# Loading the upper heads of each batch from a second DMA queue, in linear attention followed by a multiplicative FFN

## Chip, cores and metric

The kernel runs on one core of a Trainium2 chip. The metric is the time of one execution on the device, in microseconds (us); several runs give a median. One execution is also taken with the hardware profiler, and its trace is what the views below are read from.

## What is computed

The reference is linear attention with the feature map elu(x) + 1, followed by a feed-forward block in which two projections are multiplied. There are 8 batches, 8 heads, 576 positions and a head size of 64, so 4608 tokens of width 512; the hidden width is 1024. All inputs and the output are float32.

```python
def phi(x):
    return np.where(x > 0, x, np.exp(x) - 1.0) + 1.0
q_p, k_p = (phi(q), phi(k))
kv = np.einsum('bhsd,bhse->bhde', k_p, v)
z = np.sum(k_p, axis=2)
num = np.einsum('bhsd,bhde->bhse', q_p, kv)
den = np.einsum('bhsd,bhd->bhs', q_p, z)[..., None] + 1e-06
# heads are put side by side: x is 4608 x 512
a = x @ w1
b = x @ w2
h = a * b @ w3
return (h @ w_out).astype(np.float32)
```

## The kernel before, in words

Each of q, k and v of one batch is loaded into one tile of 128 partitions: heads 0 to 3 lie in partitions 0 to 63 and heads 4 to 7 in partitions 64 to 127, with nine positions of each of four heads on a partition (2304 contiguous bytes per head). `load_qkv` writes such a tile with two DMAs, one for each half of the partitions (`hh` is 0 or 1), 576 KB each. For batch 0 alone the work is cut finer: `part` 0 and 1 take two heads of each half, 288 KB per DMA. All these loads are issued from SP. Their tiles come from a pool of five (`ld`), which also holds two tiles of w3; a load waits until the tile that lay in its buffer has been read.

From a batch's tiles, ScalarE (ACT) takes the exponential, VectorE (DVE) makes phi (tiles `kphi`, `qphi`), and ACT casts v into `vt`. TensorE (PE) then forms k'v and its sums (`kv_unit`, tile `kvp`). qphi is transposed by DMA (`qt_load`, tile `qt`, two DMA transposes per batch, issued from SP), PE multiplies it with kv (`nat_unit`, tile `nd`), DVE divides (`xn`, and `xnr` for the 64 positions left over), and `xt_load` transposes the result by DMA, again from SP, into `xt`, the tokens' transposed layout that the FFN reads. Batch 0 is transposed on PE instead.

w3 and w_out are multiplied into one matrix on the chip at the start (`w3_tr`, `wf_mm`). The FFN runs over nine chunks of 512 tokens: eight `f_unit`s each (a and b, multiplied into `ab`) and four `o_unit`s, whose results (`o_sb`, four buffers) GpSimd (POOL) stores with two DMAs of 128 KB each. The weights w1, w2, w_out and w3 are loaded from POOL's queue as well, with a cast to bfloat16; the first of these DMAs is made to wait for the second part of k of batch 0 (`after(wl[0], first_loads[3])`), and the load of q of batch 1 for the second DMA of w3.

The order of all this is written out by hand: strings such as `NEXT` name the units in program order. F and O are the FFN's units, K and Q the steps of phi, V the cast of v, T `qt_load`, KV and N the attention's matrix products, X `xt_load`, and Lk, Lq and Lv the loads for the batch after next. Each engine runs its own instructions in this order.

```python
NEXT = """KV F0 Lk Ke0 F1 Ks0 Ks1 O0 N0 Ke1 Ks2 Ks3 F2 N1 O1 Lq N2 F3 N3 X0 Qe0 Qs0 Qs1
          O2 N4 X1 F4 Qe1 Qs2 O3 Lv F5 Qs3 V T F6 F7"""
```

Each DMA takes one of eight semaphores of its kind in turn (eight for the DMAs that SP and ACT issue together, eight for POOL's), so a DMA also waits until the eighth DMA before it has landed.

Of the kernel before, what the change touches and what calls it, by code (L numbers as in the profile page):

```python
# [18 lines left out]
def kernel(  # L19
# [11 lines left out]
    nc = tc.nc  # L31
# [34 lines left out]
    mm_ps = ctx.enter_context(tc.tile_pool(name="mm_ps", bufs=4, space=bass.MemoryType.PSUM))  # L66
    at_ps = ctx.enter_context(tc.tile_pool(name="at_ps", bufs=2, space=bass.MemoryType.PSUM))

    nc.scalar.preload_act_table_set("natural_log_exp_and_others")

    ident = consts.tile([P, P], BF16)
    make_identity(nc, ident)
# [19 lines left out]
    def load_qkv(name, src, b, part=None):  # L92

        if part is None or part == 0:
            raw[name, b] = ld.tile([P, 4, X], F32, tag="ld", name=f"{name}32")
        n, h0 = (4, 0) if part is None else (2, 2 * part)
        for hh in range(2):
            ins = nc.sync.dma_start(  # L98
                out=raw[name, b][hh * TP:(hh + 1) * TP, h0:h0 + n, :],
                in_=src[b, hh * 4 + h0:hh * 4 + h0 + n].rearrange("h (p j) d -> p h (j d)", j=NJ))  # L100
        return ins
# [196 lines left out]
    def after(ins, first):  # L298
        tc.add_manual_dep(ins.ins, first.ins.name, mybir.DependencyInfo(
            mybir.DependencyClass.Sync, mybir.DependencyReason.SCHED_ONLY), reason="load order")  # L300

    def load_w12(x):
        cols = slice(x * WQ, (x + 1) * WQ)
        return [nc.gpsimd.dma_start(  # L304
            out=d[:, :, cols], in_=w.rearrange("(c p) n -> p c n", p=P)[:, :, cols])
            for d, w in ((w1_sb, moe_w1), (w2_sb, moe_w2))]
# [39 lines left out]
    def load(name, b, part=None):  # L346
        return load_qkv(name, src[name], b, part)

    first_loads = [load(n, 0, i) for i in range(NI) for n in "kqv"]
    wl = [i for x in range(4) for i in load_w12(x)]  # L350
    after(wl[0], first_loads[3])
    wl += [load_wo(0), load_wo(1)]
# [131 lines left out]
```

## Time and profile before

| | |
|---|---|
| median of 3 runs | 312.65 us (312.0 to 315.04) |
| the profiled execution's own time | 312.29 us |
| its span, first to last instruction | 310.5 us |
| PE busy | 242.8 us (78%) |
| DVE busy, ACT busy | 151.6 us, 134.6 us |
| mean granted TensorE clock | 0.932 |
| moved by DMA | 51.57 MB; q1 (SP) 36.64 MB, q0 (POOL) 14.69 MB |

Times in the views are us from the start of the span unless marked ns. A row of a timeline gives start, duration, engine, line, what is written from what, and in brackets the idle time before it and what ended it. In the DMA view, q1 is the queue of SP's DMAs and q0 that of POOL's; a row has packets, MB and the time that the packets took as a share of 16 DMA engines over the stretch. Packets of one engine can overlap, so the shares may add up to over 100%. Bytes are counted as written: a cast to bfloat16 counts half of what it reads. The page's row of DMA bytes shows 173 to 261 GB/s in each of the first 27 slices of 7.76 us.

### The profile page before, as it was taken

Reading aid. Unit: us, or ns where it says so; the run is one execution under the profiler, and the core shown is the slowest. Engines: PE = TensorE matmul, PEld = TensorE weight load, DVE = VectorE, ACT = ScalarE, POOL = GpSimd, SP = SyncE. Lnnn points to the kernel's source line nnn. Section 1 sums busy time; section 2 is a strip of 40 time slices with the busy share of each in tenths; the row PEclk is TensorE's granted clock in tenths of the full one; section 3 lists DMA queues with packets and bytes.
Section 4 is the critical chain, followed back from the end, with each engine's and each line's share of the span. In section 5 each row is a group of like instructions: output and inputs, shape, how many; then the busy total and the mean of one; then the engine's idle time right before and its main releaser. Section 6 shows DMA issues by size and latency. Waiting matters only on the chain.

```text
span 310.5 us, 3924 instructions
## 1 busy us (share of the span) xinstructions
PE 242.8 (78%) x1430; PEld 116.0 (37%) x1450; DVE 151.6 (49%) x291; ACT 134.6 (43%) x187; POOL 52.4 (17%) x103
## 2 busy tenths in 40 slices
PE   0248999595197439399789999959999999999960
PEld 0223455242044114144334544524455444444420
DVE  0555404638347903379557579647755441222200
ACT  3477377725425405237505555542553333333330
POOL 2273300013000002011102112111202202203150
PEclk9999999979689958979959999997999999999995
DMA  7999999999989999999999999990781713303250
GB/s 173 229 225 198 209 237 223 214 193 261 216 170 215 211 218 187 216 204 209 204 238 213 212 221 245 218 198 9 145 108 38 144 36 68 68 2 83 52 117 20
DMA packets 56499, 51.57 MB, mean 166 GB/s; under 512 B 35744, under 2 KB 40864, under 8 KB 56480
## 3 DMA queue, kind: packets, MB, share of 16 engines
q1 hardware_dynamic: 46592, 36.64, 60.5%
q0 software_dynamic: 9888, 14.69, 22.9%
q8 instruction: 11, 0.18, 0.3%
q14 instruction: 8, 0.07, 0.1%
HBM read 38.80 MB, written 9.44 MB: 155 GB/s over the span
## 4 chain that ended last, share of the span: by engine, by line
PE 57%; DMA 31%; DVE 3%; SPq 2%; ACT 2%; issue 2%; POOL 1%; POOLq 0%; ACTq 0%; DVEq 0%
PE o_ps L286 18%; PE a_ps L267 18%; PE b_ps L267 17%; DMA qt<-qphi 9%; DMA xt<-xn 7%; DMA v<-in_v_dram 6%; DMA w3b<-in_moe_w_dram 4%; DMA w_sb<-in_moe_w_dram 3%; DMA k<-in_k_dram 3%; PE nd L179 3%; PE kvp L141 2%; SPq L98 1%; ACT vt L127 1%; DVE xn L186 1%; POOL w_sb L304 1%
## 5 line engine op out<-in xcount | busy, mean ns | idle before, releaser
L267 PE MATMUL a_ps<-xt,w_sb 128*128 128x512 bf16 x280 | 76.1, 397 | 18.3 <-DMA xt<-xn 18.2
L273 DVE TENSOR_TENSOR ab<-a_sb,b_ps 128x512 bf16<-128x512 f32 x72 | 49.3, 686 | 79.3 <-PE b_ps L267 74.8
L267 PEld LDWEIGHTS <-w_sb 128*128 128x128 bf16 x560 | 54.9, 101 | 85.0 <-issue 18.6
L267 PE MATMUL b_ps<-xt,w_sb 128*128 128x512 bf16 x280 | 75.9, 396 | 0.0
L291 POOL DMA_DIRECT2D out_dram<-o_sb x72 | 37.7, 528 | 225.8 <-ACT o_sb L289 225.8
L272 ACT COPY a_sb<-a_ps 128x512 f32<-128x512 f32 x72 | 42.0, 585 | 76.5 <-PE a_ps L267 73.5
L286 PE MATMUL o_ps<-wf_sb,ab 128*128 128x512 bf16 x272 | 69.0, 391 | 1.0 <-issue 0.2
L289 ACT COPY o_sb<-o_ps 128x512 f32<-128x512 f32 x36 | 21.0, 585 | 65.4 <-PE o_ps L286 63.4
L286 PEld LDWEIGHTS <-ab 128*128 128x128 bf16 x288 | 28.4, 101 | 33.2 <-issue 4.0
L114 DVE TENSOR_SCALAR e<-e 128x1152 bf16<-128x1152 bf16 x32 | 14.9, 467 | 29.7 <-ACT e L113 29.4
L179 PE MATMUL nd<-kv,qt 128*128 128x130 bf16 (+1 forms) x144 | 15.5, 230 | 14.6 <-DMA qt<-qphi 11.1
L117 DVE SCALAR_TENSOR_TENSOR qphi<-q,e 128x576 bf16<-128x576 f32 x32 | 23.2, 754 | 0.5
L117 DVE SCALAR_TENSOR_TENSOR kphi<-k,e 128x576 bf16<-128x576 f32 x32 | 23.0, 754 | 0.4
L113 ACT ACTIVATE e<-k 128x1152 bf16<-128x1152 f32 x16 | 18.6, 1166 | 8.1 <-DMA k<-in_k_dram 8.1
L127 ACT CAST vt<-v 128x1152 bf16<-128x1152 f32 x16 | 18.0, 1168 | 8.1 <-DMA v<-in_v_dram 8.1
L179 PEld LDWEIGHTS <-qt 128*128 128x128 bf16 (+1 forms) x144 | 10.9, 105 | 26.4 <-DMA qt<-qphi 13.1
L186 DVE TENSOR_TENSOR xn<-nd,r 128x512 bf16<-128x512 f32 x28 | 19.4, 692 | 1.0
L113 ACT ACTIVATE e<-q 128x1152 bf16<-128x1152 f32 x16 | 18.5, 1165 | 2.7 <-DMA q<-in_q_dram 2.7
L209 PE MATMUL tp<-ident,qphi 128*128 128x128 bf16 x18 | 2.3, 310 | 17.4 <-DVE qphi L117 17.4
L334 PE MATMUL wf_ps<-wo_sb,w3t 128*128 128x512 bf16 x61 | 14.8, 379 | 1.2 <-ACT w3t L329 1.0
L184 DVE TENSOR_SCALAR r<-nd 128x8 f32<-128x8 f32 (+1 forms) x36 | 5.7, 159 | 18.6 <-PE nd L179 18.6
L141 PE MATMUL kvp<-vt,kphi 64*128 64x130 bf16 x288 | 10.9, 224 | 3.3 <-ACT vt L127 3.3
(45 smaller groups left out, 96.9 us busy)
## 6 DMA issues: line engine op xcount, KB each, us to landing
out_dram<-o_sb POOLq DMA_DIRECT2D x72, 128.0 KB, 3.0
q<-in_q_dram SPq DMA_DIRECT2D x14, 576.0 KB, 11.8
k<-in_k_dram SPq DMA_DIRECT2D x14, 576.0 KB, 8.0
v<-in_v_dram SPq DMA_DIRECT2D x14, 576.0 KB, 9.8
w_sb<-in_moe_w_dram POOLq DMA_DIRECT2D x8, 256.0 KB, 9.6
w3b<-in_moe_w_dram POOLq DMA_DIRECT2D x8, 256.0 KB, 13.7
k<-in_k_dram SPq DMA_DIRECT2D x4, 288.0 KB, 6.0
q<-in_q_dram SPq DMA_DIRECT2D x4, 288.0 KB, 7.2
```

What stands on the lines that cost most here:

```text
L113: nc.scalar.activation(out=e[:, hs], in_=x[:, hs], func=AF.Exp)
L117: nc.vector.scalar_tensor_tensor(out=dst[:, h // 2, :, h % 2, :], in0=x[:, h].rearrange("p (j d) -> p j d", d=D), scalar=1.0, in1=e[:, h]. ...
L127: (copy or nc.scalar.copy)(out=vt[:, i, :, :, 0:D].rearrange("p j u d -> p u j d"), in_=raw["v", b][:, 2 * i:2 * i + 2].rearrange("p u (j ...
L141: nc.tensor.matmul(kvp[:, hh, i * KVW:(i + 1) * KVW], ph["k", b][rows, i, j].rearrange("p u d -> p (u d)"), vt[rows, i, j].rearrange("p u ...
L179: nc.tensor.matmul(nd[0:n, hp // 2, (hp % 2) * KVW:(hp % 2 + 1) * KVW], qts[b][:, hp, m * P:m * P + n], t[:, hp].rearrange("p h e -> p (h ...
L186: nc.vector.tensor_tensor(out=dst.rearrange("p (a x) e -> p a x e", a=2), in0=v4[:, :, :, 0:D], in1=r[0:n].unsqueeze(3).to_broadcast([n, 2 ...
L267: nc.tensor.matmul(ps, w[:, kc, f * P:(f + 1) * P], xt[:, 4 * c:4 * c + 4, kc, :], start=(kc == 0), stop=(kc == KC - 1))
L272: nc.scalar.copy(out=a_sb, in_=a_ps)
L273: nc.vector.tensor_mul(out=abs_[c][:, f, :], in0=a_sb, in1=b_ps)
L286: nc.tensor.matmul(o_ps, ab[:, f, m * P:(m + 1) * P], wf_sb[:, f, :], start=(f == 0), stop=(f == FC - 1))
L289: nc.scalar.copy(out=o_sb, in_=o_ps)
L291: nc.gpsimd.dma_start(out=out[b * S:(b + 1) * S, :].rearrange("(p j) n -> p j n", j=NJ)[:, j, :], in_=o_sb[i * TP:(i + 1) * TP, :])
```

## The change

The first DMA of each pair (heads 0 to 3) stays on SP. The second (heads 4 to 7, partitions 64 to 127) is issued from POOL's queue, except for part 0 of batch 0, where ACT issues it. The load of ACT's table is moved behind ACT's three DMAs.

```diff
-    nc.scalar.preload_act_table_set("natural_log_exp_and_others")
...
         for hh in range(2):
-            ins = nc.sync.dma_start(
+            ins = (nc.sync if hh == 0 else nc.scalar if (b, part) == (0, 0) else nc.gpsimd).dma_start(
                 out=raw[name, b][hh * TP:(hh + 1) * TP, h0:h0 + n, :],
                 in_=src[b, hh * 4 + h0:hh * 4 + h0 + n].rearrange("h (p j) d -> p h (j d)", j=NJ))
         return ins
...
     first_loads = [load(n, 0, i) for i in range(NI) for n in "kqv"]
+    nc.scalar.preload_act_table_set("natural_log_exp_and_others")
     wl = [i for x in range(4) for i in load_w12(x)]
     after(wl[0], first_loads[3])
```

`load_qkv` returns the second DMA of its pair, so both manual dependencies (of the first weight on k, and of q of batch 1 on w3) now hang on a DMA of POOL's own queue.

The first place is the start of the program on POOL, from the last memset to the first stores. Before (`w_sb`, `wo_sb` and `w3b` are the weights):

```order
L87 MEMSET vt 128x36
L304 DMA w_sb<-in_moe_w_dram 128x4x256 x8
L310 DMA wo_sb<-in_moe_w_out_dram 128x4x512 x2
L319 DMA w3b<-in_moe_w_dram 128x1024 x8
L236 COPY kv<-kvn 128x8x64
L237 COPY kv<-kvz 128x8
L291 DMA out_dram<-o_sb 64x512 x72
```

The same place of the changed kernel, whose lines from `load_qkv` on count one less:

```order
L86 MEMSET vt 128x36
L97 DMA k_111<-in_k_dram 64x2x576
L97 DMA q_114<-in_q_dram 64x2x576
L97 DMA v_117<-in_v_dram 64x2x576
L303 DMA w_sb<-in_moe_w_dram 128x4x256 x8
L309 DMA wo_sb<-in_moe_w_out_dram 128x4x512 x2
L318 DMA w3b<-in_moe_w_dram 128x1024 x8
L235 COPY kv<-kvn 128x8x64
L236 COPY kv<-kvz 128x8
L97 DMA q_299<-in_q_dram 64x4x576
L97 DMA k_302<-in_k_dram 64x4x576
L97 DMA v_305<-in_v_dram 64x4x576
```

Three loads of batch 0 come ahead of the weights, and the upper halves of batch 1 (`q_299`, `k_302`, `v_305`) behind all of them.

The second place is one later chunk (a pass over `NEXT`) on SP, before:

```order
L98 DMA k_1336<-in_k_dram 64x4x576 x2
L98 DMA q_1418<-in_q_dram 64x4x576 x2
L198 DMA_TRANSPOSE xt<-xn 128x16x128
L198 DMA_TRANSPOSE xt<-xnr 128x4x64
L98 DMA v_1510<-in_v_dram 64x4x576 x2
L161 DMA_TRANSPOSE qt<-qphi 128x18x64 x2
```

The same chunk on SP with the change:

```order
L97 DMA k_1336<-in_k_dram 64x4x576
L97 DMA q_1418<-in_q_dram 64x4x576
L197 DMA_TRANSPOSE xt<-xn 128x16x128
L197 DMA_TRANSPOSE xt<-xnr 128x4x64
L97 DMA v_1510<-in_v_dram 64x4x576
L160 DMA_TRANSPOSE qt<-qphi 128x18x64 x2
```

And on POOL with the change, where there were stores alone before:

```order
L97 DMA k_1336<-in_k_dram 64x4x576
L290 DMA out_dram<-o_sb 64x512 x4
L97 DMA q_1418<-in_q_dram 64x4x576
L290 DMA out_dram<-o_sb 64x512 x4
L97 DMA v_1510<-in_v_dram 64x4x576
L97 DMA k_1615<-in_k_dram 64x4x576
```

On SP one DMA of each pair is gone, and the transposes stand behind half as many loads. On POOL the other halves stand between the stores of the output, in program order.

## The prediction

> **What bounds the kernel now.** I read the page first, for its busy rows, its DMA row and its queues.
>
> ```profile
> span 310.5 us, 3924 instructions
> ...
> PE 242.8 (78%) x1430; PEld 116.0 (37%) x1450; DVE 151.6 (49%) x291; ACT 134.6 (43%) x187; POOL 52.4 (17%) x103
> ...
> DMA  7999999999989999999999999990781713303250
> ...
> q1 hardware_dynamic: 46592, 36.64, 60.5%
> q0 software_dynamic: 9888, 14.69, 22.9%
> ```
>
> The DMA row stands at 9 tenths or more from the second slice to the 27th, that is up to 210 us. The two queues' packets take 60.5% + 22.9% of 16 engines' span, against PE's 78% busy. Next I cut the span at the places where PE starts a new stage, and asked for the busy time of each.
>
> ```profile
> 24.70:63.00 38.30, 33.11 (x214) 16.67 (x217) 15.90 (x26) 24.91 (x34) 5.02 (x10) 1.00 1.15 216
> 63.00:84.50 21.50, 11.03 (x70) 5.04 (x71) 11.06 (x25) 9.19 (x11) 4.25 (x8) 0.83 1.10 228
> 84.50:113.80 29.30, 18.10 (x120) 8.66 (x121) 18.40 (x37) 8.94 (x13) 0.00 (x0) 0.85 1.01 198
> 113.80:146.90 33.10, 27.60 (x152) 12.47 (x156) 18.60 (x37) 14.64 (x19) 4.18 (x8) 0.88 1.09 208
> 146.90:176.40 29.50, 26.50 (x153) 12.34 (x156) 18.35 (x37) 13.96 (x20) 4.18 (x8) 0.88 1.02 212
> 176.40:199.70 23.30, 23.20 (x151) 11.42 (x152) 18.09 (x36) 13.19 (x18) 4.18 (x8) 1.00 1.09 231
> 199.70:228.60 28.90, 25.39 (x155) 11.99 (x158) 18.30 (x36) 13.29 (x18) 4.18 (x8) 0.94 0.66 124
> 228.60:300.40 71.80, 71.35 (x369) 33.31 (x376) 23.00 (x41) 22.84 (x40) 15.53 (x30) 1.00 0.34 67
> ```
>
> The columns are the stretch, its length, busy time and instructions of PE, PEld, DVE, ACT and POOL, the granted clock, the DMA share and GB/s. The row 176.40 to 199.70 is one whole chunk that nothing held up: 23.2 us busy of 23.3, clock 1.00. The chunks at 113.8, 146.9 and 199.7 do the same work (151 to 155 PE instructions) in 33.1, 29.5 and 28.9 us; they lose both idle time and clock. Behind 228.6 PE is busy for 71.35 of 71.8 us, and nothing there can be gained from DMA; ahead of it, DMA limits. What PE waited for is in the view of waits (total us, times, longest).
>
> ```profile
> PE a_ps L267 <- DMA xt<-xn: 18.2, 2, 9.5
> ...
> PE nd L179 <- DMA qt<-qphi: 11.1, 6, 3.5
> ...
> PE kvp L141 <- ACT vt L127: 3.3, 3, 2.6
> ```
>
> The chain of waits shows how long each such transfer was under way.
>
> ```profile
> 42.44 18.18 DMA v<-in_v_dram
> ...
> 74.57 9.86 DMA xt<-xn
> ...
> 102.56 11.12 DMA xt<-xn
> ```
>
> The 18.18 us are those of v of batch 1, most of it queue: its 1.18 MB alone are 5.4 us at the rate found below. A stall costs a second time, since PE comes out of it slow. In the timeline, four matmuls of 512 columns just before the qt stall at 127 us, and just behind it:
>
> ```profile
> 122.96 1.04 PE L267 MATMUL a_ps<-xt,w_sb 128*128 128x512 bf16 x4
> ...
> 131.91 1.91 PE L267 MATMUL a_ps<-xt,w_sb 128*128 128x512 bf16 x4
> ```
>
> 1.91 us instead of 1.04 for the same work.
>
> Why are the transfers late? In a stretch in which q1 alone worked, with loads that fill one half of the partitions at a time (50 to 53 us):
>
> ```profile
> q1 hardware_dynamic: 300, 0.65, 104.7%
> ```
>
> 300 packets, 0.65 MB in 3 us, 217 GB/s; q1's packets follow one another without a gap (104.7%). That looks like a full machine, but it isn't one. From 44 to 47 us POOL's queue still worked on w3:
>
> ```profile
> q1 hardware_dynamic: 251, 0.55, 56.2%
> q0 software_dynamic: 174, 0.30, 52.8%
> ```
>
> q1 kept 251 of its 300 packets, and 0.30 MB of q0 came on top: 0.85 MB in 3 us, 284 GB/s. Between 77 and 78 us loads on q1 met stores of the output on q0:
>
> ```profile
> DMA packets 157, 0.38 MB, mean 377 GB/s; under 512 B 22, under 2 KB 22, under 8 KB 157
> ...
> q1 hardware_dynamic: 98, 0.23, 63.6%
> q0 software_dynamic: 59, 0.15, 47.5%
> ```
>
> 377 GB/s, of which q1 has 0.23 MB, no less than alone (0.65 / 3 = 0.22). So **217 GB/s is what one queue gets with loads into one half, not what the 16 engines can move.**
>
> **The change, part by part.** Loads are 42 DMAs of 576 KB and 12 of 288 KB, 28.3 MB. At 217 GB/s they take 130 us in one queue. With the halves in two queues I expect between 217 GB/s (nothing gained) and 377 (the best stretch above); I take 340, between the 284 and the 377 and nearer to the latter, because in the 377 row q1 lost nothing, while the other has a q0 that reads twice what it writes. That makes 83 us. Transposes are the other load on q1. With almost nothing beside them (83 to 86 us):
>
> ```profile
> q1 hardware_dynamic: 1995, 0.49, 94.9%
> ```
>
> 0.49 MB in 3 us, 165 GB/s. The transposes of a batch, 590 KB of qt and 590 KB of xt, take 1.18 / 0.165 = 7.2 us. A chunk loads three tiles of 1.18 MB: before, 3.54 / 0.217 = 16.3 us, with the transposes 23.5, and with 1.05 MB of stores partly beside them more than the 23.3 us that PE needs. After: 3.54 / 0.34 + 7.2 = 17.6 us, and some 21 with stores at 0.34. **DMA then needs less than PE, and the queue empties within each chunk.** At 284 it is 12.5 + 7.2 + 3.7 = 23.4, just even.
>
> What a transpose takes with an empty queue stands in the DMA view of 215 to 235 us (issues, median us to landing):
>
> ```profile
> qt<-qphi SPq DMA_TRANSPOSE x2, 5.7
> xt<-xn SPq DMA_TRANSPOSE x1, 5.5
> ```
>
> So the sum, by stages:
> - *Start, to 24.7 us.* The loads of batch 0 moved at 238 GB/s, a little above the 217 because the short halves overlap at their borders:
>
> ```profile
> DMA packets 1161, 2.38 MB, mean 238 GB/s; under 512 B 128, under 2 KB 128, under 8 KB 1161
> ```
>
> 3.54 MB take 14.9 us at this rate, 10.4 at 340; the end comes 4.5 us earlier. The weights wait for k on POOL for 11.2 us, and ACT takes the last v at 18.83:
>
> ```profile
> POOL w_sb L304 <- DMA k<-in_k_dram: 11.2, 1, 11.2
> ...
> 18.83 1.17 ACT L127 CAST vt<-v 128x1152 bf16<-128x1152 f32 x1 [0.27 <-DMA v<-in_v_dram]
> ```
>
> On POOL k now stands first, and the weights follow when it has landed, some 4 us sooner. But three queues share the first loads, so that the first q may land no earlier. Bounds 0 and 5 us; I take 3, nearer to the 4.5.
> - *24.7 to 63.* The halves of batch 1 on SP no longer wait for w3; those on POOL stand behind the last weight, as q's second half did before. v lands well before PE asks: the 3.3 us of `kvp` go. Bounds 0 and 4; 3.
> - *63 to 84.5.* Without the v stall the first `o_unit` runs at full clock:
>
> ```profile
> 63.68 3.47 PE L286 MATMUL o_ps<-wf_sb,ab 128*128 128x512 bf16 x8
> ```
>
> Its eight matmuls take 3.47 us; at the full clock, by the pair above, about half, so 1.7 us are saved. The xt transpose takes 5.5 us instead of 9.86, so 4.4 are saved. Together 6.
> - *84.5 to 113.8.* xt 11.12 to 5.5 us: 5.6. The rest of that stall stays, since PE has work for only 11.12 - 9.5 = 1.6 us from the issue on.
> - *113.8 to 146.9, 146.9 to 176.4, 199.7 to 228.6.* The last two fall to the 23.3 us of the clean chunk: 6.2 + 5.6. Of the 9.8 us of the first I leave out two slow starts of 1.7 us: one behind the xt stall that stays, one in case the first qt still comes late. 6.4, together 18.2.
>
> 3 + 3 + 6 + 5.6 + 18.2 = 35.8. Against it I set 3 us for transposes that meet q0's loads on the engines, which the trace of before shows only with stores: at 82 to 83 us the transposes got 0.07 MB, against 0.49 / 3 = 0.16 alone.
>
> ```profile
> q1 hardware_dynamic: 260, 0.07, 35.3%
> q0 software_dynamic: 73, 0.19, 57.3%
> ```
>
> A delay of half a 576 KB load (2.7 us at 217) at each of the two xt stalls would be 3 us in all; bounds 0 and 10 (2.7 us at the two xt stalls and half of that in the three chunks that wait for qt). So 32.8 us are gained: 310.5 - 32.8 = 277.7 us of span, and with the 1.8 us that lie outside it (the execution's 312.29 - 310.5) **279.5 us**. The profiled execution is 0.4 us below the median of 312.65; that changes nothing.
>
> Costed at nothing: POOL's issues, 24 more of them. The nearest row is that of the weights (mean 798 ns for 512 rows of the tile; a load has 256):
>
> ```profile
> L304 POOL DMA_DIRECT2D w_sb<-in_moe_w_dram x8 | 6.2, 798 | 11.2 <-DMA k<-in_k_dram 11.2
> ```
>
> 24 x 0.8 = 19 us, hidden by POOL's idle time (52.4 us busy of 310.5). If that cover went, stores would be late first, and `o_sb` has four buffers. Behind an upper half that waits for its buffer on POOL stand the stores of the next `o_unit`; the buffer is freed by DVE or ACT steps that come ahead of that unit in program order, so PE doesn't wait for them. q's upper half now follows O1's stores, a third of a chunk later than the lower half, but is used a chunk later. ACT's new issues and its table load lie ahead of its first exponential:
>
> ```profile
> 0.74 1.40 SPq L98 DMA_DIRECT2D k<-in_k_dram  x2
> ...
> 0.74 1.28 ACT L69 ACT_TABLE_LOAD   x1 [0.74 <-PEq L468]
> ...
> 6.10 1.16 ACT L113 ACTIVATE e<-k 128x1152 bf16<-128x1152 f32 x1 [4.07 <-DMA k<-in_k_dram]
> ```
>
> 0.74 + 3 x 0.7 + 1.28 = 4.1 us, against 6.10; two us of cover are left, of which a k landing 1 us sooner takes one.
>
> **A rule against it.** The Trainium skill, "SBUF — State Buffer", section "Can I just issue two DMAs to hit both halves?", says no: two DMAs into the two halves at once were measured only 6% above one. Its section on the port swizzle in the same page puts 64 partitions at about 218 GB/s, and the trace agrees (217 in one queue). The 284 and 377 GB/s above speak against the first rule where the second DMA is in another queue, though no row of before has two loads of opposite halves in two queues. By the 6%, the time would be that of the first rival.
>
> **The rivals.**
> - *Nothing gained in the rate* (a queue more, the same engines). For it: q1's packets already fill the engines' time, 104.7%. Against it: the 377 GB/s. Then the rate stays between 217 and the 238 of the start, the waits above (18.2 + 11.1 + 3.3 us) shrink by a tenth at most, some 3 us, and the start gains an issue or two of 0.7: 307 to 312 us. Chance 0.09. The Trainium skill's rule above is this case.
> - *Half the gain*, a rate like the 284: queues empty only at the end of a chunk. The v wait goes, xt and qt land 2 to 3 us sooner in place of 4 to 5, and half of the clock loss stays: some 20 us, 287 to 296. Chance 0.22.
> - *Slower:* transposes starve. On SP a transpose had to wait only for loads issued ahead of it; now q0 can hold an upper v and the next k, issued later, which the engines serve in turn with it. If the engines' rate stays at 217 and the turn is by packets (256 bytes against 2304), a transpose ends only with q0's 1.18 MB, 5.4 us later. It decides as soon as such a delay is longer than what the halved loads ahead of it save (2.7 us); over the two xt and four qt, the clean chunk's among them, that is 6 x 2.7 = 16 us, and 328 us. The row at 82 us speaks for the turn, the 377 against the fixed rate. Chance 0.06.
>
> **Chances and range.** Forecast (266 to 287) 0.63, half 0.22, nothing 0.09, slower 0.06. The upper end reaches through the second rival to 300. The lower takes the start at 5, no loss to q0, the first of the three chunks clean, all the idle time of the second stage (38.3 - 33.1 = 5.2 in place of 3), and xt stalls too short for the clock to fall: 279.5 - 2 - 3 - 3.4 - 2.2 - 3.4 = 265.5, rounded to 266. A run of this kernel tells 1% (3 us) from nothing. Faster by over that 0.87, within it 0.07, slower 0.06.
>
> **What would show it.** Right: in the row of stretches, over 300 GB/s wherever loads run; 23.3 us for the chunk in which N0 waited; xt in 5.5 to 7 us; v no longer in the chain; a DMA row with gaps ahead of 200 us. Wrong: 217 GB/s with both queues busy; q1 transposes whose landing grows; PE idle behind `o_ps` because POOL sits on a load.

## Result and the profile after

The change made the kernel slower: 324.46 us (322.23 to 328.27, four runs) against 313.16 us of the kernel before in the same runs (312.0 to 315.04), a ratio of 1.033 with a 95% interval of 1.025 to 1.042. Times here and below are medians of all runs, while ratios compare the means of those runs that lie within 1.5% of the fastest of their kernel (one run of `first_only`, at 433.95 us, lies far outside). The forecast was 279.5 us, with a range of 266 to 300; it was wrong, and in the sign too. The profiled execution took 324.24 us. From the page of the changed kernel, the rows that answer to those shown of before:

```profile
span 322.5 us, 3954 instructions
...
DMA  7999999999899999996999999699177260321324
...
q0 software_dynamic: 13152, 27.96, 42.7%
q1 hardware_dynamic: 40016, 22.48, 39.8%
```

The bytes were moved as intended: q0 now carries 27.96 MB in place of 14.69, q1 22.48 in place of 36.64. The DMA row stands at 9 tenths in 24 of its first 28 slices, now of 8.06 us each: up to 226 us in place of 210. The limit that was to go away lasts longer than before. The view of waits shows where PE pays:

```profile
PE nd L178 <- DMA qt<-qphi: 29.6, 10, 8.2
...
PE a_ps L266 <- DMA xt<-xn: 8.7, 2, 4.4
...
PE w3p L327 <- DMA w3b<-in_moe_w_dram: 3.3, 1, 3.3
```

The wait for xt fell from 18.2 to 8.7 us, as forecast. The wait for qt rose from 11.1 to 29.6 us and ate twice that, and a wait for w3 (before its transposition on PE, `w3p`) rose from 0.6 to 3.3 us. In the DMA view of the whole span, the median time from issue to landing of the 14 transposes into qt says the same thing in one row. First before, then after:

```profile
qt<-qphi SPq DMA_TRANSPOSE x14, 7.1
```

```profile
qt<-qphi SPq DMA_TRANSPOSE x14, 11.1
```

The chain of waits names the worst of them. In the kernel before it has three over 5 us:

```profile
121.62 10.05 DMA qt<-qphi
...
149.90 6.62 DMA qt<-qphi
...
199.94 9.95 DMA qt<-qphi
```

In the changed kernel it has six, of 8.29 to 18.97 us; the three longest:

```profile
61.48 12.51 DMA qt<-qphi
...
89.64 18.97 DMA qt<-qphi
...
186.21 14.04 DMA qt<-qphi
```

The following table puts the first `kvp` matmul of batches 1 to 7 side by side, from the timelines (us from the span's start). The last column is an experiment from below, `two_dma`, for comparison.

| mark | before | after | `two_dma` |
|---|---|---|---|
| batch 1 | 61.9 | 64.4 | 58.0 |
| batch 2 | 91.2 | 96.4 | 81.4 |
| batch 3 | 121.3 | 128.6 | 102.6 |
| batch 4 | 146.9 | 155.5 | 124.4 |
| batch 5 | 176.4 | 186.1 | 149.1 |
| batch 6 | 199.7 | 218.6 | 172.5 |
| batch 7 | 228.5 | 244.5 | 195.9 |
| last copy into `o_sb` | 300.4 | 316.4 | 267.7 |
| end of span | 310.5 | 322.5 | 277.9 |

The change loses 1 to 3 us in each stage up to batch 5, and 9.2 us from batch 5 to 6: the chunk that nothing held up before (23.3 us) now takes 32.5. These are two rows of the stretches of the changed kernel (columns as in the prediction):

```profile
186.10:218.60 32.50, 25.07 (x153) 11.81 (x156) 18.30 (x36) 13.31 (x18) 5.51 (x10) 0.89 0.99 174
218.60:244.50 25.90, 23.52 (x151) 11.32 (x152) 18.11 (x36) 13.30 (x18) 4.20 (x8) 1.00 0.62 127
```

In the first, the DMA share is 0.99 and yet only 174 GB/s are moved, less than the 217 of one queue. The engines are full, of something slow. The second is shorter than before (25.9 against 28.8 us). 4 us come back behind the last store (4.2 us from the end of its issue to the end of the span, against 8.2), for which I have no cause.

**What the engines do then.** I cut the transposes at 89.64, the 18.97 us of the chain, into pieces of 3 us. One from the middle, 96 to 99 us, and one from behind the loads, 105 to 108 us (packets, MB, share of 16 engines):

```profile
q0 software_dynamic: 135, 0.55, 95.3%
q1 hardware_dynamic: 137, 0.04, 10.2%
```

```profile
q1 hardware_dynamic: 1804, 0.51, 122.1%
q0 software_dynamic: 19, 0.05, 6.4%
```

The two queues get the same number of packets, 135 and 137 (112 and 116 in the piece before, 144 and 141 in the next; from 90 to 93 us it was even 143 to 35). But a packet of q0 carries 0.55 MB / 135 = 4.1 KB on average (in the trace 4608 bytes, two rows, with some packets of 4 bytes between them), and one of the transposes 256 bytes. So q1 moves 0.04 MB in 3 us; as soon as q0 is empty it makes 1804 packets and 0.51 MB in the same time. The Trainium skill, "DMA: Bandwidth & Descriptors", section "Queues, rings and completion order", says that each DMA engine serves the queues that have work in turn and changes at packet borders; the equal counts here agree. Whether the packets that the profile counts are those of that page isn't shown.

The stall at 186.21 us looks different. From 189 to 192 us:

```profile
q0 software_dynamic: 78, 0.29, 103.4%
q1 hardware_dynamic: 434, 0.11, 34.4%
```

Here the transposes get more than five packets for one of q0, and still only 0.11 MB in 3 us (0.10 in the next 3 us). That transposes are slow while q0's loads are under way holds for both stalls; turns one for one are shown for the longest alone.

What q0 has to do at that moment stands in the timeline of POOL and of SP:

```profile
88.16 0.62 POOL L97 DMA_DIRECT2D k<-in_k_dram  x1
90.47 0.62 POOL L97 DMA_DIRECT2D q<-in_q_dram  x1 [1.69 <-issue]
```

```profile
87.18 12.94 SPq L160 DMA_TRANSPOSE qt<-qphi  x2
100.22 3.32 SPq L97 DMA_DIRECT2D k<-in_k_dram  x1
```

From 86.29 to 91.1 us POOL issues five upper halves, 2.95 MB, of batches 3 and 4; the first step that reads any of them, the exponential of k of batch 3, starts at 111.69 us. They stand beside the transposes of batch 2, issued at 87.18, for which PE waits. In SP's single queue they would have come behind. SP itself sits in the two transposes for 12.94 us (3.82 before) and issues its next loads so much later, so that here the opposite halves do not run together. SP's issuing alone doesn't explain the slow transposes: it ends at 100.12 us, and from 100.1 to 102 us the counts are still 91 and 91.

At the start the same turn meets the weights. Between 24 and 27 us:

```profile
q1 hardware_dynamic: 255, 0.55, 85.8%
q0 software_dynamic: 255, 0.12, 30.8%
```

Batch 1's lower halves no longer wait behind w3 on their own queue, and take 255 of 510 packets beside the weights, whose packets are the small ones here (0.12 MB / 255 = 0.5 KB). PE's first matmul on w3 waits 3.3 us for it.

### The profile page after: what moved, and what is told of

It reads as the page before. It is cut to its first block, busy times and chain, and to the rows that moved or that the text cites. A ratio compares the mean times of both kernels' runs of the same rounds, so it can differ in the third digit from the quotient of the medians.

```text
span 322.5 us, 3954 instructions
## 1 busy us (share of the span) xinstructions
PE 247.6 (77%) x1430; PEld 117.9 (37%) x1450; DVE 151.2 (47%) x291; ACT 134.6 (42%) x187; POOL 67.6 (21%) x127
## 3 DMA queue, kind: packets, MB, share of 16 engines
q0 software_dynamic: 13152, 27.96, 42.7%
q1 hardware_dynamic: 40016, 22.48, 39.8%
## 4 chain that ended last, share of the span: by engine, by line
PE 48%; DMA 37%; issue 4%; DVE 3%; ACT 3%; SPq 2%; POOL 2%; POOLq 0%; ACTq 0%; DVEq 0%
DMA qt<-qphi 22%; PE o_ps L285 16%; PE a_ps L266 15%; PE b_ps L266 14%; DMA w3b<-in_moe_w_dram 6%; DMA q<-in_q_dram 3%; DMA k<-in_k_dram 3%; PE nd L178 3%; DMA w_sb<-in_moe_w_dram 3%; SPq L160 2%; ACT e L112 1%; PE kvp L140 1%; DVE qphi L116 1%; DVE e L113 1%; ACT vt L126 1%
## 5 line engine op out<-in xcount | busy, mean ns | idle before, releaser
L266 PE MATMUL a_ps<-xt,w_sb 128*128 128x512 bf16 x280 | 79.3, 409 | 11.5 <-DMA xt<-xn 8.7
L266 PEld LDWEIGHTS <-w_sb 128*128 128x128 bf16 x560 | 56.1, 103 | 81.5 <-issue 17.4
L266 PE MATMUL b_ps<-xt,w_sb 128*128 128x512 bf16 x280 | 76.8, 399 | 0.0
L285 PE MATMUL o_ps<-wf_sb,ab 128*128 128x512 bf16 x272 | 67.8, 386 | 1.1 <-issue 0.4
L178 PE MATMUL nd<-kv,qt 128*128 128x130 bf16 (+1 forms) x144 | 16.6, 240 | 32.3 <-DMA qt<-qphi 29.6
L112 ACT ACTIVATE e<-q 128x1152 bf16<-128x1152 f32 x16 | 18.5, 1166 | 1.9 <-DMA q<-in_q_dram 1.8
## 6 DMA issues: line engine op xcount, KB each, us to landing
v<-in_v_dram SPq DMA_DIRECT2D x7, 576.0 KB, 10.7
w_sb<-in_moe_w_dram POOLq DMA_DIRECT2D x8, 256.0 KB, 10.8
```

Source lines behind the costliest of these rows:

```text
L112: nc.scalar.activation(out=e[:, hs], in_=x[:, hs], func=AF.Exp)
L178: nc.tensor.matmul(nd[0:n, hp // 2, (hp % 2) * KVW:(hp % 2 + 1) * KVW], qts[b][:, hp, m * P:m * P + n], t[:, hp].rearrange("p h e -> p (h ...
L266: nc.tensor.matmul(ps, w[:, kc, f * P:(f + 1) * P], xt[:, 4 * c:4 * c + 4, kc, :], start=(kc == 0), stop=(kc == KC - 1))
L285: nc.tensor.matmul(o_ps, ab[:, f, m * P:(m + 1) * P], wf_sb[:, f, :], start=(f == 0), stop=(f == FC - 1))
```

## The experiments

My theory after this reading: writing both halves at once is faster, but the split breaks the order of one queue, and transposes in packets of 256 bytes starve beside loads in packets of 4608. The rivals: the start (weights, ACT's issues) makes the loss; the rate doesn't rise at all; POOL's queue or POOL's stores are at fault. Each ratio is to the kernel before, in runs on the same chip, with its 95% interval.

**The parts of the change.** `first_only` splits batch 0 alone:

```diff
-            ins = (nc.sync if hh == 0 else nc.scalar if (b, part) == (0, 0) else nc.gpsimd).dma_start(
+            ins = (nc.sync if hh == 0 or b > 0 else nc.scalar if part == 0 else nc.gpsimd).dma_start(
```

> Only batch 0 is split over the queues; all later loads are on SP as before. Theory (the engines take turns between q1 and q0 packet by packet, so the transposes' small packets starve beside q0's loads): batch 0 has no DMA transposes, so nothing starves; the first FFN matmul comes near 26 us as in the changed kernel against 24.7, and the time stays within 1% of before, 311 to 316 us. Rival (the halves are late because POOL's queue holds them behind other work): the same, since nothing is behind them. Third view (the loss is mostly the start): 318 us or more.

312.76 us, 0.999 (0.995 to 1.003), with the first FFN matmul at 25.90 us, as in the changed kernel (25.94). `pool_b2` is the kernel before with only the upper halves of batches 2 to 7 on POOL:

```diff
-            ins = nc.sync.dma_start(
+            ins = (nc.sync if hh == 0 or b < 2 else nc.gpsimd).dma_start(
```

> The split for batches 2 to 7 alone; batches 0 and 1 as before. Theory of the turns: the waits for qt stay as long as in the changed kernel (25 to 30 us in total against 11.1), so most of the loss stays: 318 to 326 us. If the loss were the start's: 311 to 315 us or faster than before.

321.2 us, 1.027 (1.023 to 1.031). So the start is neutral as a whole, and most of the loss of 3.3% lies in the loads that meet transposes.

**Without small packets.** In `plain_before` and `plain_after` each DMA transpose of the kernel before and of the changed one is a plain copy of the same bytes into the same tile; what they compute goes on from untransposed data. The core of the edit:

```diff
-                out=t[:, hh * NI:(hh + 1) * NI].rearrange("p i (j t) -> p (i j) t", t=TP),
-                in_=ph["q", b][hh * TP:(hh + 1) * TP].rearrange("p i j u d -> p (i j u d)"),
-                transpose=True)
+                out=t[hh * TP:(hh + 1) * TP].rearrange("p c s -> p (c s)"),
+                in_=ph["q", b][hh * TP:(hh + 1) * TP].rearrange("p i j u d -> p (i j u d)"))
```

> The kernel before with each DMA transpose replaced by a plain DMA copy of as many bytes between the same tiles (rows of 1 to 4 KB instead of 256-byte packets); the attention and FFN then compute on data that isn't transposed. It is the reference for the next run. By bytes, 8.3 MB at some 217 GB/s instead of 165 save 12 us of DMA: 297 to 304 us.

> The changed kernel with the same copies in place of the transposes. Theory of the turns: with large packets q1 gets its bytes' share of the turns, the starving goes, and the higher rate of two halves at once is left: faster than the copies on the kernel before by 2% to 6%, 282 to 296 us. Rival (POOL's order, loads behind stores and buffers): POOL's queue is the same, so it stays slower than the copies on the kernel before by some 3%. Third (two queues add no rate): the same within 1%.

294.29 us, 0.943 (0.937 to 0.949), and 303.14 us, 0.961 (0.952 to 0.970). Both missed: the first is below its 297 us, and the second should have been the faster one. Two things may have spoilt the pair: a copy into partitions 64 to 127 writes the half that q0's loads write, and batch 1 differs too. `copy_before` and `copy_b2` take both away: the copy into qt is one DMA over all 128 partitions, and the split is that of `pool_b2`. These also go on from untransposed data; the diff stands against `plain_before`.

```diff
-        for hh in range(2):
-            nc.sync.dma_start(
-                out=t[hh * TP:(hh + 1) * TP].rearrange("p c s -> p (c s)"),
-                in_=ph["q", b][hh * TP:(hh + 1) * TP].rearrange("p i j u d -> p (i j u d)"))
+        nc.sync.dma_start(
+            out=t.rearrange("p c s -> p (c s)"),
+            in_=ph["q", b].rearrange("p i j u d -> p (i j u d)"))
```

> As the run with copies on the kernel before, but the copy for qt is one DMA over all 128 partitions, so that it writes both halves alike, as the transposes do. Reference for the next run: 288 to 295 us.

> The same copies in the kernel with the split for batches 2 to 7. Theory of the turns (small packets): faster than the reference of this pair by 1% to 5%, since packets of 4 KB against 4 KB share the engines evenly, and the rate of two halves is left. A wider theory (any DMA on q1 loses to loads on q0 that are issued later, whatever its packets): still slower than the reference, by 1% to 3%. Rival (POOL's order): the same as this, but then the qt copies land as fast as in the reference, and PE waits for loads instead.

297.24 us, 0.946 (0.938 to 0.955), and 298.04 us, 0.951 (0.944 to 0.958). The reference is 2 us above its range, and the split kernel is neither faster, as the theory of the turns had it, nor clearly slower, as the wider theory had it. With transposes the split costs 2.7%, with copies nothing that can be told from noise. So POOL's queue and its order alone don't make the loss; but a copy differs from a DMA transpose in more than the size of its packets, and the pair doesn't tell the two apart. The view of DMA of `copy_b2`, 99 to 102 us, opposite halves in two queues:

```profile
DMA packets 280, 0.88 MB, mean 294 GB/s; under 512 B 21, under 2 KB 21, under 8 KB 280
...
q0 software_dynamic: 140, 0.57, 65.1%
q1 hardware_dynamic: 140, 0.31, 37.2%
```

294 GB/s, where one half alone gets 217: the rate rises by a third when both are under way. The equal counts also bear on its size. q0 writes 0.57 MB / 3 us = 190 GB/s, nearly all that one half takes, and q1, with as many but smaller packets, is at little more than half of it. That the turns tie q1 to q0's count is argued from this, not tested.

**The order given back.** In `hold` batches 2 to 7 are split as in `pool_b2`, but an upper half on POOL waits until the transposes ahead of it in program order have landed (k and v behind qt, q behind xt):

```diff
+                ins = (nc.gpsimd if upper else nc.sync).dma_start(
...
+                if upper and last:
+                    after(ins, last[-1])
```

> Batches 2 to 7 split over SP and POOL as in the change, batches 0 and 1 as before; but each upper half on POOL waits until the transposes that stand ahead of it in program order have landed (k and v behind qt, q behind xt). Theory of the turns: with no loads on q0 beside the transposes these go at full speed again, and the two halves overlap at about 290 GB/s: the waits for qt fall below 6 us and the time below that of before, 292 to 306 us. Rival (POOL's order): the upper halves come later still, so slower than the split without the wait, 322 us or more. Third (two queues add no rate): 308 to 316.

307.66 us, 0.984 (0.975 to 0.993): the wait alone turns 2.7% of loss into 1.6% of gain, less than the 292 to 306 us expected. From its DMA view of the whole span:

```profile
qt<-qphi SPq DMA_TRANSPOSE x14, 7.8
```

The landing is back near the 7.1 us of before. PE's wait for qt, expected below 6 us, is 13.7 us in the profiled execution (311.06 us), against 11.1 before and 29.6 in the changed kernel. One reason why the gain stays small is that the held half often runs after the other. Between 132 and 135 us q0 is alone, at 0.60 MB / 3 us = 200 GB/s:

```profile
q0 software_dynamic: 148, 0.60, 99.7%
```

**Another second queue.** `act_queue` issues the upper halves of batches 2 to 7 from ACT:

```diff
-            ins = nc.sync.dma_start(
+            ins = (nc.sync if hh == 0 or b < 2 else nc.scalar).dma_start(
```

> The kernel of before, with the upper halves of batches 2 to 7 issued from ACT's queue instead of POOL's. On POOL's queue a load's packets carry 4.1 KB, on SP's and, I expect, on ACT's 2.3 KB. If the transposes lose because the engines take one packet of each queue in turn, they still meet a second queue here, with packets of 2304 bytes against 256, so that a 590 KB pair of transposes passes while nine times as many bytes of loads pass, unless these end first: slower than before, less than or like the 1.027 with POOL: 1.00 to 1.03, 313 to 322 us, with qt and xt waits that name the DMA and not an engine. ACT's program order is another cost: a load that waits for its buffer stops ACT's casts and exponentials, up to 5 us a chunk. If instead only POOL's queue is at fault (its software queue, its larger packets), the time falls to 285 to 305 us, since both halves run together.

320.6 us, 1.022 (1.014 to 1.030). So a second queue that isn't POOL's costs time as well. But the traces don't show the same cause. The median landing is that of `first_only`, which loses nothing (8.2 us too):

```profile
qt<-qphi SPq DMA_TRANSPOSE x14, 8.2
```

PE's wait for qt is 12.3 us, near the 11.1 of before; the one for xt is 24.1 us, against 18.2. ACT's loads travel in packets of 2304 bytes, one row, and there are no equal counts in the stretches of 3 us from 84 to 102 us: q1, with the transposes, has 77 packets to 243 of ACT's queue from 87 to 90 us, but 1780 to 61 from 93 to 96. ACT's program order, in which the loads now stand between casts and exponentials, may be what costs. How much of the 2.2% is which isn't settled here, and neither is whether starving for long needs POOL's queue with its larger packets.

**Both halves in one queue.** `short_pieces` leaves all loads on SP and cuts each into four DMAs of 288 KB that alternate between the halves; `one_head` cuts into eight of 144 KB:

```diff
-        for hh in range(2):
+        for a in range(h0, h0 + n, 2):
+            for hh in range(2):
...
-                out=raw[name, b][hh * TP:(hh + 1) * TP, h0:h0 + n, :],
+                    out=raw[name, b][hh * TP:(hh + 1) * TP, a:a + 2, :],
...
-                in_=src[b, hh * 4 + h0:hh * 4 + h0 + n].rearrange("h (p j) d -> p h (j d)", j=NJ))
+                    in_=src[b, hh * 4 + a:hh * 4 + a + 2].rearrange("h (p j) d -> p h (j d)", j=NJ))
```

> The kernel before, all loads on SP, but each cut into four DMAs of 288 KB that alternate between the halves, as batch 0 already has it. The transposes keep their place in one queue; the halves overlap at the borders, 238 instead of 217 GB/s. If the limit is the half that is written: 12 us less DMA up to 210 us, 300 to 306 us. If the queue itself is limited to 217: 312 to 315 us, or slower by SP's 42 more issues.

> The kernel of before, all loads on SP, each load cut into eight DMAs of one head and one half (144 KB), the halves in alternation; the cut into four of 288 KB gave 0.965. If the gain there comes from both halves being under way at once in one queue, a finer alternation gives at least as much: 0.95 to 0.965, 297 to 302 us, and over 230 GB/s where loads run alone. Against it stand SP's issues, about 0.6 us each, 336 loads in place of 168 (about 200 us of SP's time, 25 or so DMAs a chunk) and the eight semaphores, which let only eight DMAs or 1.15 MB be under way and hold back the transposes behind them. If these bind, the time goes back up to 305 to 325 us, with PE's waits on xt and qt larger than the 18.0 and 10.4 us of the coarser cut.

302.74 us, 0.965 (0.956 to 0.973), and 312.5 us, 0.998 (0.994 to 1.002). The finer cut was expected to be the faster one and is not, but its rate is the telling number. In `one_head`, 50 to 53 us, where the kernel before had 217 GB/s:

```profile
DMA packets 441, 0.82 MB, mean 274 GB/s; under 512 B 90, under 2 KB 90, under 8 KB 440
...
q1 hardware_dynamic: 437, 0.80, 102.7%
```

274 GB/s in one queue. What eats it is SP's issuing, as its timeline shows:

```profile
107.20 3.07 SPq L199 DMA_TRANSPOSE xt<-xn  x1
110.37 6.14 SPq L99 DMA_DIRECT2D q<-in_q_dram  x8
116.61 1.20 SPq L199 DMA_TRANSPOSE xt<-xnr  x1
117.90 5.03 SPq L99 DMA_DIRECT2D v<-in_v_dram  x8
123.04 4.31 SPq L162 DMA_TRANSPOSE qt<-qphi  x2
```

Eight issues of q hold SP for 6.14 us and eight of v for 5.03, and the transposes stand behind them: once issued, those of qt land in 4.6 us (median), and yet PE waits 16.2 us for them.

**One DMA over both halves.** Even heads go to partitions 0 to 63 and odd heads to 64 to 127 from batch 1 on, so that 128 partitions have one stride in the source; the division writes `xn` with the heads back in order. `one_dma` loads a tile in one DMA, `two_dma` in two of two heads per half:

```diff
+        if b > 0:
+            v = src[b].rearrange("(x a) (p j) d -> (a p) x (j d)", a=2, j=NJ)
+            for x in (0, 2):
+                ins = nc.sync.dma_start(out=raw[name, b][:, x:x + 2], in_=v[:, x:x + 2])
+            return ins
...
-            out=dst.rearrange("p (a x) e -> p a x e", a=2), in0=v4[:, :, :, 0:D],
+            out=dst.rearrange("p (a x) e -> p a x e" if b == 0 else "p (x a) e -> p a x e", a=2),
+            in0=v4[:, :, :, 0:D],
```

> All on SP, as before, but from batch 1 on each of q, k and v is one DMA of 1.18 MB over all 128 partitions in place of two of 576 KB over 64: even heads go to partitions 0 to 63, odd heads to 64 to 127, so that source and tile have one uniform stride, and the division writes xn with the heads put back in order. The number of SP's load issues from batch 1 on is halved. Theory (the rate is set by how many partitions are written at once, and one queue in its order serves the transposes best): if the DMA's packets are spread over the engines by partition, both halves are written all the time, as with one-head pieces (274 GB/s in one queue), without their issue cost; the kernel beats the cut into four (0.965): 0.93 to 0.965, 290 to 302 us, with 260 to 300 GB/s where loads run alone. If each engine works through the partitions in the same order, the engines write one half and then the other, the rate stays at 210 to 230 GB/s and the time at 308 to 314 us.

> As one_dma, but each tile in two DMAs of two heads of each half (590 KB each, 128 partitions), so as many issues as before. By the theory the rate is that of one_dma and the transposes and first steps of phi wait for less at a time (k's exponential of the first two slots needs the first DMA only, as far as the waits follow the parts of the tile): within 1.5% of one_dma, 288 to 302 us. If the spread over the engines is what fails in one_dma, it fails here too: 306 to 314 us.

281.15 us, 0.897 (0.891 to 0.903), and 279.64 us, 0.893 (0.885 to 0.900): the fastest version of this study, and both below the least that was expected (290 and 288 us). In `two_dma`, 50 to 53 us:

```profile
DMA packets 531, 1.17 MB, mean 389 GB/s; under 512 B 31, under 2 KB 31, under 8 KB 530
...
q1 hardware_dynamic: 530, 1.15, 102.3%
```

389 GB/s with one queue working. The 217 were the rate of loads into half of the partitions, not of one queue. Then the stretches of `two_dma` from batch 4 on:

```profile
124.40:149.10 24.70, 23.54 (x153) 11.46 (x152) 18.22 (x37) 14.02 (x20) 4.18 (x8) 1.00 0.94 263
149.10:172.50 23.40, 23.40 (x154) 11.47 (x154) 18.09 (x36) 13.19 (x18) 4.18 (x8) 1.00 0.87 244
172.50:195.90 23.40, 23.40 (x155) 11.48 (x156) 18.09 (x36) 13.18 (x18) 4.18 (x8) 1.00 0.56 124
```

PE is busy for 23.40 of 23.40 us at full clock in two chunks running, and for 23.54 of 24.70 in the one ahead of them. PE's two waits shrink from 18.2 and 11.1 us to these (in `one_dma` they are 4.0 and 3.3):

```profile
PE a_ps L273 <- DMA xt<-xn: 7.0, 2, 4.3
...
PE nd L184 <- DMA qt<-qphi: 4.1, 2, 2.9
```

**The second queue by itself.** `two_dma_pool` differs from `two_dma` only in the queue of the second DMA of each pair, for batches 2 to 7. Both queues write both halves:

```diff
-                ins = nc.sync.dma_start(out=raw[name, b][:, x:x + 2], in_=v[:, x:x + 2])
+                ins = (nc.gpsimd if x and b > 1 else nc.sync).dma_start(
+                    out=raw[name, b][:, x:x + 2], in_=v[:, x:x + 2])
```

> two_dma with its second DMA of each pair (two heads of each half, 128 partitions) on POOL's queue for batches 2 to 7. Both halves are written at once by either queue alone, so a second queue has no rate to give: what it does now is the split by itself. If the loss of the change comes from the order (transposes of small packets in turn with loads issued later on the other queue), this kernel is slower than two_dma's 279.6 us although its loads are as fast: by 3 to 10 us, 283 to 290 us, with the qt and xt waits of PE above two_dma's 4.1 and 7.0 us, less than the change's loss since the loads that the transposes meet end sooner at 390 GB/s. If the loss came only from the rate when both queues write one half, or from POOL's stores, it is within 1% of 279.6 us, or up to 2% faster because SP issues fewer DMAs.

302.39 to 313.27 us, median 310.96, against 279.42 to 279.97 for `two_dma`. The sign is as expected, the size is two to three times the expected 3 to 10 us: even the lowest of the four is 22.7 us above. The two kernels ran on different chips, on which the kernel before took 314.54 and 313.21 us. The four runs spread over 11 us, and the profile is of the run of 309.48 us, so its rows needn't hold in full for the one of 302.39. From its view of waits, its DMA view of the span, and the queues at 84 to 87 us:

```profile
PE nd L185 <- DMA qt<-qphi: 24.4, 10, 6.3
```

```profile
qt<-qphi SPq DMA_TRANSPOSE x14, 11.4
```

```profile
q0 software_dynamic: 185, 0.75, 98.5%
q1 hardware_dynamic: 166, 0.04, 6.2%
```

The picture of the change again, 166 packets for 185 and 0.04 MB for 0.75, and 11.4 us of landing in place of 5.5, where the rate in either queue is high. A second queue on POOL costs by itself; the rate and the half that it writes are not what makes the loss.

## Why the prediction was wrong, by its own steps

- **What bounds the kernel.** Right. DMA limits up to batch 7, PE behind it: 71.9 us from batch 7 to the last copy in both kernels, 71.8 in `two_dma`. (In the rows of before, one of the slices that the prediction has at 9 tenths or more is at 8, and the GB/s of the first 27 slices run from 170, not 173, to 261. Neither changes the argument.)
- **217 GB/s as one queue's rate with loads into one half.** Half right. It is the rate of the half; the queue has no part in it (389 GB/s in one queue over both halves). The prediction read the rise in its rows of two queues as the gain of a second queue, but in these rows q0 moved w3, over 128 partitions, or stores, not loads into one half.
- **340 GB/s with the halves in two queues.** Too high: 260 to 302 GB/s in pieces of 3 us in which opposite halves run together (260 from 123 to 126 us in the changed kernel, 302 from 96 to 99 us in `copy_b2`), and about 200 where one queue is alone, which is much of the time, since SP and POOL don't keep step. "DMA then needs less than PE" rested on the 340 and fell with it; the lower bound of 217 was nearer.
- **The +3 us for transposes that meet q0's loads.** This is the step that failed. It counted half a load at the two xt stalls, some 1.5 us each, had qt only in its upper bound, and bounded the whole at 10 us. The xt stalls shrank as forecast; it was qt that paid. The median landing of qt grew by 4.0 us, single ones took 12.51, 18.97 and 14.04 us against the 5.7 us assumed, and PE waited 18.5 us more for qt, and was busy for 4.8 us more (247.6 in place of 242.8) with the same 1430 instructions. The row that it used (0.07 MB of transposes in 1 us at 82 to 83 us) was of short stores that soon end; it held two queues at work together, but not a queue of 2.95 MB behind it. The prediction also let POOL run ahead by one v and one k; the timeline shows five halves.
- **The stages.** Start: 3 us of gain expected, the first FFN matmul came 1.3 us later (25.94 against 24.68), and `first_only` was neutral. To 63 us: v is no longer in the chain, as forecast, but w3 and q took over (19.62 and 10.09 us in the chain, the 3.3 us for w3, the 255 to 255 packets), and the stretch took 38.5 us in place of 37.2. xt: 10 us expected, 9.5 gained in PE's waits. The three chunks: 18.2 expected; the middle chunk that was to stay at 23.3 lost 9.2, and only the last gained, 2.9 of 5.6.
- **The sum itself.** It described `two_dma`. From 310.5 to 277.9 us of span are 32.6 us, for 32.8 expected. Part of that agreement is luck: the 32.8 had 3 us taken off for q0's loads, which `two_dma` doesn't have, and its first stages gave 3.9 us in place of 6. By stage it is 3.9 up to batch 1, 18.6 from there to batch 4 (18 expected), 4.8 (6.2), -0.1 (0) and 5.4 (5.6). The full clock behind stalls that are gone came as argued (1.00 in every stretch of `two_dma` from batch 2 on). What was wrong is the means: the gain belongs to both halves at once and an order kept in one queue.
- **The rivals.** Slower by starving transposes, 328 us, was nearest to the 324.46, at a chance of 0.06. That q0 holds loads issued later and that transposes are slow beside them is shown; that the time comes so near is in part luck. Its 16 us were 2.7 us at each of six stalls, the two of xt among them. Measured, the waits for xt fell by 9.5 us, and those for qt alone rose by 18.5, for 10.8 expected. Its condition, an unchanged 217 GB/s, isn't needed, since the loss comes with the higher rate as well (`two_dma_pool`). It deserved far more, because the one row that bore on it (82 to 83 us) spoke for it.
- **The rule against it.** The Trainium skill, "SBUF — State Buffer", section "Can I just issue two DMAs to hit both halves?", gives 6% for two DMAs into two halves. Measured were about 200 GB/s with one queue alone and 260 to 302 with both under way, so the 6% is too low here; but its advice, that only one transfer over all 128 partitions reaches all ports, agrees with the 389 GB/s and the fastest kernel. The prediction weighed its figure and passed over its advice.

Still open: what slows the transposes where the counts aren't equal, whether packet size alone does it, how much of the loss of `act_queue` is ACT's order, why the tail of the changed kernel is 4 us shorter, and what spreads the runs of `two_dma_pool`.

## What to carry to other kernels

A second DMA queue was no second machine here. In the longest stall it got as many packets as the first (135 to 137), so that transposes on the critical path, in small packets, starved beside large loads that were not needed yet, and the priority that one queue's order gives was lost. Look at packets per queue, not only at bytes. Before splitting a load over queues, see which partitions it writes: if it covers half of them, a layout that lets one DMA cover all 128 gave 389 GB/s for 217, and 10.7% of the time, in the old order. A term that is bounded at 10 us from a stretch with short stores isn't bounded for a queue that runs far ahead; ask what the other engine can have issued by then.

## What the runs showed of the hardware beyond the forecast

- One queue moved 389 GB/s into 128 partitions and 217 into 64, with the same packets of 2304 bytes; alternating pieces of 144 KB got 274.
- In the traces, POOL's loads of 2304-byte rows travel in packets of 4608 bytes, two rows; those of SP and ACT in packets of 2304, one row.
- Beside a busy second queue (POOL's) the issue itself of two DMA transposes held SP for 12.94 us, against 3.82 in the same place before.
